# A windowed-attention and MLP kernel: one evacuation of k split by PSUM bank, small matmul groups and two stores put at other places

## The chip, the cores and the metric

The kernel runs on one core of a Trainium2 chip. Its engines have an instruction stream each and run side by side, held together by semaphores: PE (TensorE, matrix products into PSUM), DVE (VectorE), ACT (ScalarE), POOL (GpSimd) and SP (SyncE, which here issues every DMA). PSUM has eight banks of 512 fp32 values in each of 128 partitions. The metric is the device time of one execution in microseconds (us); lower is better.

## The reference

All data is bf16, S = 2048 rows of D = 512. `A` is attention in which each row sees itself and seven earlier rows two apart, with 32 heads of 16; `B` is a mixer with an MLP of width 1376. Both start from the same normalised rows, and the outcome is `x + A * silu(B)`.

```python
xn = layernorm(x)
# A: windowed attention
qkv = (xn @ wqkv) -> q, k, v of 32 heads x 16
idx = pos[:, None] - 2 * arange(8)           # masked where negative
attn = softmax(einsum("bhsd,bhswd->bhsw", q, k[idx]) * 16**-0.5)
s = einsum("bhsw,bhswd->bhsd", attn, v[idx]).reshape(B, S, D) @ wo
# B: mixer and MLP
h  = gelu(layernorm(xn) @ w1)
hs = concat(quarters of h shifted by +1, -1, +2, -2 rows) @ w2
x1 = xn + hs
g  = silu(x1 + gelu(layernorm(x1) @ w3) @ w4)
out = x + s * g
```

## The kernel before

The rows are split by parity: p = 0 holds the even rows, p = 1 the odd ones, 1024 each, so that a window two rows apart becomes eight neighbours within one parity. The row chunks c = 0 to 3 have 512 rows (0 and 1 of parity 0, 2 and 3 of parity 1), and 16 row tiles of 128.

The order of the instructions is written out by hand; each engine takes its own in the order in which the program names them. The first part (to about 109 us) makes q, k, v, the mixer and the first MLP product for all chunks. PSUM banks 0 to 5 serve it as three pairs in turn (`pair`, L91): a pair is filled by eight products of PE (`proj`, L332, products on L337) and emptied by ACT or DVE, and PE needs the same pair again three pairs later.

`k_all` (L358) makes k. The scores later want k twice, once with the odd heads of each pair set to zero and once with the even ones, as alternate elements of one tile, `kM[..., e]` with e = 0, 1. So each pair of banks is copied out twice, with a mask `em[:, e]` as scale. On ACT both copies are L366. In one call, `k_all(2, (1,), both=False)` (L596), the copy e = 0 is on ACT and the copy e = 1 on DVE (L368). Behind that call stand `w1(2, 0)`, `w1(2, 1)` and `w1(3, 0)`, whose products are also on L337.

The second part (109 us to 181 us) runs the attention in 18 units (`for n in range(NU)`, L900), nine for each parity, each of 114 rows. A unit n consists of

- `scores(n)` (L640): 32 small products on PE (L647) into banks 0 to 3, then the Exp on ACT (L654);
- `band(n - 1)` (L656): the mask on DVE (L659), for most units one unit later;
- `values(n - 2)` (L664): 32 small products (L673) into bank 4 and 16 (L683) that sum the weights into bank 5, then a copy of bank 4 by ACT (L688). For n = 15 both `values(13)`, ahead of the scores, and `values(14)` are called, and from then on `values(n - 1)`;
- a share of about nine products of `g_w4` (L779, products on L785). This is the MLP's second product: 16 groups of 11 products into one bank, 6 or 7, and then taken up by DVE (L798) and ACT (L805, or L801);
- one small group of four products: `g_v` (units 0 to 7, products on L816, copied by ACT, L385) or `g_fin` (from unit 8, L826, products on L838). `g_fin` is the output projection of one row tile: ACT copies the bank (L845), DVE multiplies by the gate (L853) and adds x (L855), and every second tile SP stores 256 KB (`store`, L749).

`w4_take` (L885) hands out the w4 products: three calls in a unit, about a third of its quota `q` each. Where a w4 group ends inside the second or third call, the unit's small group (`extra`) is run there, and the next w4 group starts behind it. The final steps of a `g_fin` group (L853, L855) wait in `finals` and are flushed at the start of the next unit, in unit 16 in its middle. Its store waits in `stores`, and `flush_stores(n - 2)` issues what is at least two units old.

The weights of the softmax are inverted for batches of four units (`inverse`, L695). They go to DRAM (`write_rec`, L700, DMAs on L704), come back spread over the partitions (`read_rec`, L706, DMAs on L707) and are multiplied in by DVE (`apply`, L712, product on L720). The values of each unit are loaded by `load_va` (L633, DMA on L636) into one of three slots.

After unit 17: `values(17)`, the last eight w4 products, two expansions of the last inverses on PE (L726), their copies on ACT (L734), and then seven `g_fin` tiles of parity 1 one after the other (L984), each with its two DVE products, and six stores. Each of these loops ends with `flush_stores(n)`.

Of the kernel before, what the change touches and what calls it, by code (L numbers as in the profile page):

```python
# [8 lines left out]
AF = mybir.ActivationFunctionType  # L9
ALU = mybir.AluOpType  # L10
# [10 lines left out]
def kernel(  # L21
# [17 lines left out]
    PE, DVE, ACT, POOL, SP = nc.tensor, nc.vector, nc.scalar, nc.gpsimd, nc.sync  # L39

    def pin(ins):

        return tc.keep_in_program_order(ins)
# [6 lines left out]
    NF = (F + P - 1) // P  # L50
# [11 lines left out]
    NU = 2 * UP  # L62
# [19 lines left out]
    def b8(shape, name):  # L82
        return big.tile(shape, BF16, name=name, tag="b8")
# [32 lines left out]
    for h in range(2):  # L116
        pin(SP.dma_start(
            out=wqk_sb[:, :, h * D // 2 : (h + 1) * D // 2], in_=wqkv_v[:, :, h * D // 2 : (h + 1) * D // 2]
# [31 lines left out]
    em = const.tile([P, 2], F32, name="em")  # L150
# [62 lines left out]
    class Norm:  # L213
# [24 lines left out]
        def apply(self, lo, hi):  # L238
            for j in range(lo, hi):
                pin(DVE.tensor_scalar(  # L240
                    out=self.dst[:, j, :], in0=self.src[:, j, :], scalar1=self.mv[:, j, 0:1],
                    scalar2=self.rstd[:, j : j + 1], op0=ALU.subtract, op1=ALU.mult,
                ))
# [88 lines left out]
    def proj(c, a, w, rhs):  # L332
        pt = pair()
        for b in range(2):
            nt = 2 * a + b
            for dt in range(ND):
                pin(PE.matmul(  # L337
                    pt[:, b, :], lhsT=w[:, dt, nt * P : (nt + 1) * P], rhs=rhs[:, dt, :],
                    start=(dt == 0), stop=(dt == ND - 1),
                ))  # L340
        return pt

    def chunk(t, c):
        p, k = c // 2, c % 2
        return t[p][:, :, k * CH : (k + 1) * CH]
# [12 lines left out]
    def k_all(c, parts=(0, 1), both=True):  # L358

        p, k = c // 2, c % 2  # L360
        for a in parts:
            pt = proj(c, a, wqk_sb[:, :, D : 2 * D], chunk(xnT, c))
            for e in range(2):
                dst = kM[p][:, 2 * a : 2 * a + 2, 8 + k * CH : 8 + (k + 1) * CH, e]
                if e == 0 or both:
                    pin(ACT.activation(dst, pt, AF.Copy, scale=em[:, e : e + 1]))  # L366
                else:
                    pin(DVE.tensor_scalar(out=dst, in0=pt, scalar1=em[:, e : e + 1], scalar2=None, op0=ALU.mult))  # L368

    vn = {"n": 0}  # L370

# [214 lines left out]
    while vputs:  # L586
# [11 lines left out]
        out=w4_sb[:, 0 : NF - 1, :],  # L598
# [65 lines left out]
    def values(n):  # L664
        p, u = n // UP, n % UP
        if u == 0:
            oT[p] = b8([P, ND, MQ], f"oT{p}")
        pr = probs.pop(n)
        for dt in range(ND):
            for k in range(2):  # L670
                for rg in range(4):
                    x = (2 * dt + k) * QB
                    pin(PE.matmul(  # L673
                        O_ps[32 * rg : 32 * rg + 32, x : x + QB],
                        lhsT=va_r[:, n % NV, k, 32 * (4 * dt + rg) : 32 * (4 * dt + rg) + 32],
                        rhs=pr[:, rg, x : x + QB], start=True, stop=True, tile_position=(0, 32 * rg),
                    ))
        b = batch_of[n]
        lo, hi = batches[b]
        st = den_st if hi - lo == 4 else den_s2  # L680
        for dt in range(ND):
            for rg in range(4):
                pin(PE.matmul(  # L683
                    D_ps[32 * rg : 32 * rg + 32, :], lhsT=st[:, 4 * (n - lo) + dt, :],
                    rhs=pr[:, rg, dt * NQ : (dt + 1) * NQ], start=(n == lo and dt == 0),
                    stop=(n == hi - 1 and dt == ND - 1), tile_position=(0, 32 * rg),
                ))
        pin(ACT.activation(  # L688
            oT[p][:, :, u * NQ : (u + 1) * NQ], O_ps[:, 0 : ND * NQ].rearrange("p (a q) -> p a q", q=NQ), AF.Copy
        ))  # L690
# [132 lines left out]
    stores = []  # L823
    now = {"n": 0}

    def g_fin(p, i, st=None, n=2, half=False, later=None, parts=1):  # L826

        W = D // parts
        sg = {}

        def one(pt, k):
            h, dt = k // ND, k % ND
            c = slice(h * W, (h + 1) * W)
            if dt == 0:
                sg["no"] = free.pop(0) if h else None
            if h:
                pt = PS[:, sg["no"], :]
            pin(PE.matmul(  # L838
                pt[:, 0:W], lhsT=oT[p][:, dt, i * P : (i + 1) * P], rhs=wo["sb"][:, dt, c],
                start=(dt == 0), stop=(dt == ND - 1),  # L840
            ))
            if dt == ND - 1:
                if h == 0:
                    sg["t"] = fin.tile([P, D], BF16, name="sg", tag="f")
                pin(ACT.activation(sg["t"][:, c], pt[:, 0:W], AF.Copy, scale=2.0 if half else 1.0))  # L845
                if h:
                    free.append(sg["no"])

        def done(pt):
            t = sg.pop("t")  # L850

            def steps():
                pin(DVE.tensor_tensor(out=t, in0=t, in1=xn[p][:, i, :], op=ALU.mult))  # L853
                x_o = xo[p][:, i, :]
                pin(DVE.tensor_tensor(out=x_o, in0=t, in1=x_o, op=ALU.add))  # L855
                if st is not None:
                    stores.append((now["n"], lambda: store(st, p, i + 1 - n, n)))

            if later is None:
                steps()  # L860
            else:
                later.append(steps)

        return Group(ND * parts, one, done)
# [10 lines left out]
    def flush(q):  # L875
        while q:
            q.pop(0)()

    def flush_stores(n):
        while stores and stores[0][0] <= n:  # L880
            stores.pop(0)[1]()

    open_w4 = [g for g in w4s]

    def w4_take(k, extra=()):  # L885

        while k > 0 and open_w4:
            k -= open_w4[0].take(k)
            if open_w4[0].at == open_w4[0].n:
                open_w4.pop(0)  # L890
                if extra:
                    extra.pop(0).all()

    HEAD, LAST = 6, 8
    W4 = 16 * NF - LAST - HEAD
    given = 0
    xo_at = {9: (1, 0), 12: (1, 2), 13: (1, 4), 16: (1, 6)}
    ends = {5: 0, 9: 1, 13: 2, 16: 3}
    load_va(0)
    for n in range(NU):  # L900
        now["n"] = n
        q = W4 * (n + 1) // NU - given
        given += q
        extra = small_g.get(n, [])
        if n == 0:
            w4_take(HEAD)

        for j in range(2):
            if n == NU - 1:
                read_rec(3, 2 * j, 2)  # L910
            elif n - 1 - j in ends:
                read_rec(ends[n - 1 - j], 2 * j, 2)
        if n == 15:
            values(13)
        scores(n)
        if 1 <= n < 16:
            band(n - 1)
        if n >= 2 and n != 15:
            values(n - 2 if n < 16 else n - 1)
        if n + 1 < NU:  # L920
            load_va(n + 1)
        if n == 4:
            load_wo()
        if n != 16:
            flush(finals)
        if n in ends:
            recs[ends[n]] = inverse()
            write_rec(ends[n])
        if n == 17:
            free += [2, 3]  # L930
            pin(ACT.preload_act_table_set("silu_and_others"))
        w4_take(q // 3)
        late = list(gates)
        gates.clear()
        flush(tanhs)
        if n == 15:
            apply(2, 0, 2)
        if n == 17:
            band(n)
        w4_take(q // 3, extra)  # L940
        if n < 15:
            flush(late)
        if 15 <= n < 17:
            band(n)
        if n == 16:
            flush(finals)
        if n == 15:
            values(14)
        w4_take(q - 2 * (q // 3), extra)
        for j in range(2):  # L950
            if n < 15 and n - 2 - j in ends:
                apply(ends[n - 2 - j], 2 * j, 2)
        if n == 16:
            apply(2, 2, 2)
        if n >= 15:
            flush(late)
            flush(gates)
        while extra:
            extra.pop(0).all()

        flush(vstores)
        if n in xo_at:
            load_xo(*xo_at[n])
        if n != 15:
            flush_stores(n - 2)

    n = NU
# [4 lines left out]
        apply(3, j, 2)  # L972
    flush(gates)
    flush(tanhs)
    w4_take(LAST)
    flush(tanhs)
    banks = [PS[:, i, :] for i in range(2)]
    for j in range(2):
# [4 lines left out]
        apply_kept(NU - 2 + j, kept[j])  # L983
    for i in range(1, 8):  # L984
        g_fin(1, i, (SP if i % 2 or i == 6 else None), 1 if i >= 6 else 2, half=i >= 5, parts=1 if i < 4 else 2).all()
        flush_stores(n)


# [28 lines left out]
```

## Time and profile before

| | us |
|---|---|
| three runs: median, lowest, highest | 193.91, 193.33, 194.72 |
| the profiled execution: device time | 194.53 |
| the profiled execution: span in the trace | 192.6 |
| last matmul of PE ends | 188.0 |
| last DVE product ends | 189.8 |
| last store is issued | 189.8 |

How to read the profile: it is one execution. The page gives each engine's busy time, the DMA queues, and the costliest groups by source line, with the idle time just ahead of them and what ended it ("issue" is time in which the profile shows nothing that the engine waited for). The views of the trace used below are the timeline (start, duration, engine, line, operation, output and inputs, count of merged instructions, and in brackets the idle time ahead of the row with its releaser), the waits (engine, line, releaser: total us, times, longest), and the windows (for a stretch of time, the busy us and the count of PE, PE's weight load, DVE, ACT and POOL, then the granted clock of PE, the DMA engines' busy share and GB/s).

In the first part and the units, the costliest groups are these (busy us, mean ns of one):

| group | count | us | ns |
|---|---|---|---|
| PE L479, w3 | 176 | 38.3 | 379 |
| PE L785, w4 | 176 | 46.2 | 380 |
| ACT L654, Exp | 18 | 30.4 | 1688 |
| ACT L366, copies of k | 15 | 19.5 | 1400 |
| DVE L659, mask | 18 | 19.9 | 1103 |
| DVE L368, copy of k | 1 | 1.4 | 1361 |

Products of PE overlap; one of 512 columns follows the other every 0.216 us.

### The profile page before, as it was taken

What the parts mean: (1) busy time and instruction counts of PE and PEld (TensorE: products, weight loads), DVE (VectorE), ACT (ScalarE), POOL (GpSimd) and SP (SyncE); (2) the same over time, 40 slices, a digit from 0 to 9 for tenths busy, and PEclk for the clock granted to TensorE, in tenths of its full rate; (3) what the DMA queues carried; (4) which work ended last, traced back from release to release, by engine and by line L of the source; (5) the groups of instructions that cost most, each with busy time, mean ns of one, the idle gap of its engine ahead of it and who ended that gap; (6) DMA issues with size and microseconds to landing.
All of it is one profiled execution on the core that took longest, in us unless ns stands there. A gap on an engine that the chain in (4) does not pass through costs nothing.

```text
span 192.6 us, 5267 instructions
## 1 busy us (share of the span) xinstructions
PE 185.7 (96%) x2244; PEld 90.2 (47%) x2244; DVE 114.5 (59%) x226; ACT 132.2 (69%) x152; POOL 20.4 (11%) x60
## 2 busy tenths in 40 slices
PE   7999999999999999999999999999999999989990
PEld 2464444444444444444444444544454555444570
DVE  5897783222562996665000045665579789779694
ACT  7299858977268246165656788787778878876881
POOL 3025653000020022042000000000000000000000
PEclk9999999999999999999999999999999999999997
DMA  4999574589704113514700045357653753744724
GB/s 138 326 359 296 132 150 95 95 258 340 238 0 82 32 29 64 104 27 83 223 25 0 26 144 161 108 165 239 212 161 78 220 195 84 205 115 101 226 74 149
DMA packets 39859, 27.74 MB, mean 144 GB/s; under 512 B 18068, under 2 KB 39324, under 8 KB 39836
## 3 DMA queue, kind: packets, MB, share of 16 engines
q1 hardware_dynamic: 39836, 27.41, 51.9%
q8 instruction: 17, 0.28, 0.6%
q14 instruction: 6, 0.05, 0.1%
HBM read 17.14 MB, written 6.59 MB: 123 GB/s over the span
## 4 chain that ended last, share of the span: by engine, by line
PE 75%; ACT 8%; DMA 6%; DVE 6%; issue 1%; SPq 1%
PE PS L479 20%; PE PS L785 18%; PE PS L337 14%; ACT kM L366 7%; PE PS L439 5%; PE PS L816 4%; PE PS L838 3%; PE PS L673 3%; PE PS L647 3%; PE PS L374 3%; DMA ring<-rec_d 3%; DMA xn<-in_A_x_dram 2%; PE PS L683 2%; DVE sg L853 2%; DMA rec_d<-rec 1%
## 5 line engine op out<-in xcount | busy, mean ns | idle before, releaser
L479 PE MATMUL PS<-x1nT,w_sb 128*128 128x512 bf16 (+1 forms) x176 | 38.3, 379 | 0.0
L654 ACT ACTIVATE prob<-PS 128x1824 bf16<-128x1824 f32 x18 | 30.4, 1688 | 4.4 <-PE PS L647 3.6
L785 PE MATMUL PS<-w_sb,h3a 128*128 128x512 bf16 x128 | 32.7, 380 | 0.0
L485 ACT ACTIVATE h3a<-PS 128x1024 bf16<-128x1024 f32 x16 | 16.4, 1025 | 20.6 <-PE PS L479 20.6
L798 DVE TENSOR_TENSOR xn<-PS,xn 128x512 bf16<-128x512 f32 x15 | 10.3, 687 | 31.8 <-PE PS L785 31.5
L479 PEld LDWEIGHTS <-w_sb 128*128 128x128 bf16 (+1 forms) x176 | 17.6, 100 | 20.4
L337 PE MATMUL PS<-xnT,wqk_sb 128*128 128x512 bf16 x112 | 25.0, 379 | 0.1
L366 ACT ACTIVATE kM<-PS,em 128x1024 bf16<-128x1024 f32 x15 | 19.5, 1400 | 2.2 <-PE PS L337 2.1
L659 DVE TENSOR_TENSOR prob<-prob,maskb 128x1824 bf16<-128x1824 bf16 x18 | 19.9, 1103 | 1.3 <-ACT prob L654 1.3
L785 PEld LDWEIGHTS <-h3a 128*128 128x128 bf16 x128 | 11.3, 97 | 13.4 <-issue 1.2
L337 PEld LDWEIGHTS <-wqk_sb 128*128 128x128 bf16 x112 | 10.9, 98 | 13.2 <-issue 0.3
L838 PE MATMUL PS<-wo_sb,oT 128*128 128x512 bf16 (+1 forms) x80 | 15.5, 336 | 0.0
L447 DVE TENSOR_TENSOR xn<-PS,xn 128x1024 bf16<-128x1024 f32 x8 | 9.6, 1214 | 9.6 <-PE PS L439 9.6
L337 PE MATMUL PS<-xn2T,w_sb 128*128 128x512 bf16 x64 | 14.6, 379 | 0.2 <-DVE kM L368 0.2
L439 PE MATMUL PS<-w_sb,hT 128*128 128x512 bf16 x64 | 14.5, 379 | 0.1
L845 ACT ACTIVATE sg<-PS 128x512 bf16<-128x512 f32 (+1 forms) x20 | 10.1, 512 | 6.2 <-PE PS L838 5.9
L785 PE MATMUL PS<-w_sb,h3b 128*128 128x512 bf16 (+1 forms) x48 | 13.5, 381 | 0.0
L385 ACT ACTIVATE vst<-PS 128x512 bf16<-128x512 f32 (+1 forms) x12 | 8.9, 738 | 5.3 <-ACT sig L805 3.0
L412 ACT ACTIVATE hT<-PS 128x1024 bf16<-128x1024 f32 x8 | 8.0, 1028 | 5.6 <-PE PS L337 5.6
L224 DVE BATCH_NORM_STATS2 l1s<-xn 128x6 f32<-128x512 bf16 x16 | 10.2, 679 | 1.3 <-DMA xn<-in_A_x_dram 1.3
L838 PEld LDWEIGHTS <-oT 128*128 128x128 bf16 x80 | 7.8, 98 | 6.2 <-issue 0.3
L224 DVE BATCH_NORM_STATS2 l3s<-xn 128x6 f32<-128x512 bf16 x16 | 10.2, 683 | 0.2
(105 smaller groups left out, 221.8 us busy)
## 6 DMA issues: line engine op xcount, KB each, us to landing
ring<-v_d SPq DMA_DIRECT2D x18, 256.0 KB, 3.0
v_d<-vst SPq DMA_DIRECT2D x16, 256.0 KB, 3.1
xo<-in_A_x_dram SPq DMA_DIRECT2D x8, 256.0 KB, 3.6
ring<-rec_d SPq DMA_DIRECT2D x8, 228.0 KB
out_dram<-xo SPq DMA_DIRECT2D x7, 256.0 KB, 6.6
xn<-in_A_x_dram SPq DMA_DIRECT2D x6, 256.0 KB, 4.7
w_sb<-in_B_w_dram SPq DMA_DIRECT2D x1, 1376.0 KB
w_sb<-in_B_w_dram SPq DMA_DIRECT2D x1, 1280.0 KB
```

What stands on the lines that cost most here:

```text
L224: pin(DVE.bn_stats(out=self.st[:, j, :], in_=self.src[:, j, :]))
L337: pin(PE.matmul(pt[:, b, :], lhsT=w[:, dt, nt * P : (nt + 1) * P], rhs=rhs[:, dt, :], start=(dt == 0), stop=(dt == ND - 1),))
L366: pin(ACT.activation(dst, pt, AF.Copy, scale=em[:, e : e + 1]))
L439: pin(PE.matmul(pt[:, j, :], lhsT=w2_src(p, g, m0), rhs=w2_sb[:, g, :], start=(g == 0), stop=(g == ND - 1),))
L479: pin(PE.matmul(pt[:fs, ft % 2, :], lhsT=w3_sb[:, dt, ft * P : ft * P + fs], rhs=x1nT[:, dt, :], start=(dt == 0), stop=(dt == ND - 1),))
L485: pin(ACT.activation(t[:, o : o + 2, :], pt, AF.Gelu_apprx_tanh))
L654: pin(ACT.activation(pr, S_ps[:, :, 0 : ND * NQ], AF.Exp, scale=SCALE))
L659: pin(DVE.tensor_tensor(out=f, in0=f, in1=maskb[:], op=ALU.min))
L785: pin(PE.matmul(pt, lhsT=h3_of(c, ft)[:fs, jj * P : (jj + 1) * P], rhs=w4_sb[:fs, ft, :], start=(ft == 0), stop=(ft == NF - 1 and silu < 2),))
L798: pin(DVE.tensor_tensor(out=x_i, in0=pt, in1=x_i, op=ALU.add))
L838: pin(PE.matmul(pt[:, 0:W], lhsT=oT[p][:, dt, i * P : (i + 1) * P], rhs=wo["sb"][:, dt, c], start=(dt == 0), stop=(dt == ND - 1),))
L845: pin(ACT.activation(sg["t"][:, c], pt[:, 0:W], AF.Copy, scale=2.0 if half else 1.0))
```

## The change

Four edits, in one step:

1. In the call of `k_all` with `both=False`, the copies are split by bank and not by e: ACT copies the first bank of the pair for e = 0 and for e = 1, DVE the second.
2. In unit 15, `values(14)` is called behind the first share of w4 products and not behind the second.
3. `w4_take` has a budget for the unit (`unit["left"]`). In units 0 to 7, if a w4 group has ended, its `g_v` group has run, and three or fewer products of the unit's budget are left, the unit ends there, and what is left goes into the next unit's quota. From unit 8 on, the `g_fin` group no longer runs where a w4 group ends, but at the end of the unit, after the w4 shares. Up to unit 16, if the w4 group open at that point has between one and four products done, it is first taken on to five.
4. In unit 17 no stores are flushed. In the end's loop, after tile 1, its store is put at the head of the list, so that the two stores of xo0 still in the list come behind it.

On the engines' queues this gives: on PE, another order of the groups in units 1, 2, 6 to 8, 11 to 13 and 15 to 17, with the same instructions; on DVE, two copies of 128x512 in place of one of 128x1024, and the second half of the product with the weights of batch 2 (L720) ahead of L853 and L855 of the last parity-0 tile; on ACT, two copies of 128x512 in place of one of 128x1024; on SP, the first xo1 store ahead of the last two xo0 stores, behind the two L707 reads of the last batch.

```diff
@@ -362,10 +362,12 @@
             pt = proj(c, a, wqk_sb[:, :, D : 2 * D], chunk(xnT, c))
             for e in range(2):
                 dst = kM[p][:, 2 * a : 2 * a + 2, 8 + k * CH : 8 + (k + 1) * CH, e]
-                if e == 0 or both:
-                    pin(ACT.activation(dst, pt, AF.Copy, scale=em[:, e : e + 1]))
+                sc = em[:, e : e + 1]
+                if both:
+                    pin(ACT.activation(dst, pt, AF.Copy, scale=sc))
                 else:
-                    pin(DVE.tensor_scalar(out=dst, in0=pt, scalar1=em[:, e : e + 1], scalar2=None, op0=ALU.mult))
+                    pin(ACT.activation(dst[:, 0], pt[:, 0], AF.Copy, scale=sc))
+                    pin(DVE.tensor_scalar(out=dst[:, 1], in0=pt[:, 1], scalar1=sc, scalar2=None, op0=ALU.mult))

     vn = {"n": 0}

@@ -882,28 +884,40 @@

     open_w4 = [g for g in w4s]

+    unit = {"left": 0, "given": 0}
     def w4_take(k, extra=()):

+        k = min(k, unit["left"])
         while k > 0 and open_w4:
-            k -= open_w4[0].take(k)
+            t = open_w4[0].take(k)
+            k -= t
+            unit["left"] -= t
+            unit["given"] += t
             if open_w4[0].at == open_w4[0].n:
                 open_w4.pop(0)
                 if extra:
                     extra.pop(0).all()
+                    if unit["left"] <= 3:
+                        k = unit["left"] = 0

     HEAD, LAST = 6, 8
     W4 = 16 * NF - LAST - HEAD
-    given = 0
     xo_at = {9: (1, 0), 12: (1, 2), 13: (1, 4), 16: (1, 6)}
     ends = {5: 0, 9: 1, 13: 2, 16: 3}
     load_va(0)
     for n in range(NU):
         now["n"] = n
-        q = W4 * (n + 1) // NU - given
-        given += q
+        q = W4 * (n + 1) // NU - unit["given"]
         extra = small_g.get(n, [])
+        early = n < 8
         if n == 0:
+            unit["left"] = HEAD
             w4_take(HEAD)
+            unit["given"] = 0
+        unit["left"] = q

         for j in range(2):
             if n == NU - 1:
@@ -934,19 +948,21 @@
         gates.clear()
         flush(tanhs)
         if n == 15:
+            values(14)
             apply(2, 0, 2)
         if n == 17:
             band(n)
-        w4_take(q // 3, extra)
+        w4_take(q // 3, extra if early else [])
         if n < 15:
             flush(late)
         if 15 <= n < 17:
             band(n)
         if n == 16:
             flush(finals)
-        if n == 15:
-            values(14)
-        w4_take(q - 2 * (q // 3), extra)
+        w4_take(q - 2 * (q // 3), extra if early else [])
+        if not early and n < NU - 1 and 0 < open_w4[0].at < 5:
+            unit["left"] = 5 - open_w4[0].at
+            w4_take(unit["left"])
         for j in range(2):
             if n < 15 and n - 2 - j in ends:
                 apply(ends[n - 2 - j], 2 * j, 2)
@@ -961,7 +977,7 @@
         flush(vstores)
         if n in xo_at:
             load_xo(*xo_at[n])
-        if n != 15:
+        if n != 15 and n < NU - 1:
             flush_stores(n - 2)

     n = NU
@@ -972,7 +988,8 @@
         apply(3, j, 2)
     flush(gates)
     flush(tanhs)
-    w4_take(LAST)
+    unit["left"] = 16 * NF
+    w4_take(16 * NF)
     flush(tanhs)
     banks = [PS[:, i, :] for i in range(2)]
     for j in range(2):
@@ -983,6 +1000,8 @@
         apply_kept(NU - 2 + j, kept[j])
     for i in range(1, 8):
         g_fin(1, i, (SP if i % 2 or i == 6 else None), 1 if i >= 6 else 2, half=i >= 5, parts=1 if i < 4 else 2).all()
+        if i == 1:
+            stores.insert(0, stores.pop())
         flush_stores(n)


```

## The prediction

> **What bounds the kernel now.** I read the page first: which engine is busy, and from when to when.
>
> ```profile
> PE 185.7 (96%) x2244; PEld 90.2 (47%) x2244; DVE 114.5 (59%) x226; ACT 132.2 (69%) x152; POOL 20.4 (11%) x60
> ...
> q8 instruction: 17, 0.28, 0.6%
> ```
>
> PE (TensorE) is busy 96% of a span of 192.6 us, so only what makes PE wait, or what lies behind its last matmul, can be worth anything. The second view is therefore the waits of PE from 12 us on: two in all.
>
> ```profile
> PE PS L673 <- issue: 0.5, 1, 0.5
> PE PS L337 <- DVE kM L368: 0.2, 1, 0.2
> ```
>
> The timeline shows the second of them, at 46 us. ACT's third copy of k (L366) ends at 44.92 (42.29 + 2.63), DVE's one copy (L368) starts only then and ends at 46.32, and PE, which wants that pair of PSUM banks again, starts 0.21 us late:
>
> ```profile
> 42.29 2.63 ACT L366 ACTIVATE kM<-PS,em 128x1024 bf16<-128x1024 f32 x2
> ...
> 44.96 1.36 DVE L368 TENSOR_SCALAR kM<-PS,em 128x1024 bf16<-128x1024 f32 x1 [3.17 <-ACT kM L366]
> ...
> 46.38 0.38 PE L337 MATMUL PS<-xn2T,w_sb 128*128 128x512 bf16 x1 [0.21 <-DVE kM L368]
> ```
>
> The timeline of PE shows the first, in unit 16: values(15) runs 21 of its 32 products, stops for 0.53 us with no releaser, then runs the other 11. All 32 read one loaded tile and one PSUM bank, so no data can have arrived between the 21st and the 22nd.
>
> ```profile
> 168.26 0.42 PE L673 MATMUL PS<-prob,ring 128*32 128x57 bf16 x32
> 168.51 0.39 PE L683 MATMUL PS<-prob,den_st 128*32 128x114 bf16 x16
> 168.83 0.82 PE L785 MATMUL PS<-w_sb,h3a 128*128 128x512 bf16 x3
> 169.49 1.03 PE L838 MATMUL PS<-wo_sb,oT 128*128 128x512 bf16 x4
> 170.45 0.40 PE L647 MATMUL PS<-qT,kM 32*128 32x57 bf16 x32
> 170.78 0.35 PE L673 MATMUL PS<-prob,ring 128*32 128x57 bf16 x21
> 171.66 0.27 PE L673 MATMUL PS<-prob,ring 128*32 128x57 bf16 x11 [0.53 <-issue]
> ```
>
> Last, the end. DVE waits 1.10 us for the read of the last weights (L707), then has no idle time until its last product at 189.80. The last store is issued at 189.83 and the span ends 2.8 us later.
>
> ```profile
> 176.52 1.24 SPq L707 DMA_DIRECT2D ring<-rec_d  x2
> ...
> 177.81 12.37 SPq L749 DMA_DIRECT2D out_dram<-xo  x7
> ...
> 181.52 1.31 DVE L720 TENSOR_TENSOR oT<-oT,ring 128x912 bf16<-128x912 bf16 x2 [1.10 <-DMA ring<-rec_d]
> ```
>
> The windows of 1 us say what room the DMA engines have there (the last two columns are their busy share and GB/s):
>
> ```profile
> 180.00:181.00 1.00, 1.00 (x7) 0.44 (x5) 0.42 (x1) 1.00 (x3) 0.00 (x0) 1.00 1.00 344
> ...
> 186.00:187.00 1.00, 1.00 (x12) 0.89 (x10) 0.93 (x4) 0.89 (x3) 0.00 (x0) 1.00 0.76 254
> 187.00:188.00 1.00, 1.00 (x10) 0.69 (x7) 0.97 (x3) 0.90 (x3) 0.00 (x0) 1.00 0.46 152
> 188.00:189.00 1.00, 0.04 (x1) 0.00 (x0) 0.97 (x4) 0.40 (x2) 0.00 (x0) 1.00 0.36 119
> 189.00:190.00 1.00, 0.00 (x0) 0.00 (x0) 0.77 (x3) 0.00 (x0) 0.00 (x0) 1.00 0.86 287
> ```
>
> **Part 1, the copies of k.** One ACT copy of 1024 columns (2.63 / 2 = 1.31 us) and one DVE copy (1.36) become two of 512 on each. The two engines then write different blocks of kM, where now they write alternate elements of one, so DVE need not wait for ACT. A 512-column copy from PSUM takes ACT 0.60 where 1024 take 1.025 (L796 and L348), so splitting adds about 0.17: ACT ends at 45.1 instead of 44.92. The next ACT copy, of hT, slips by that; the one after it waits 0.41 us for PE anyway and hides it, and without that cover it would cost 0.17. DVE can start when PE fills the second bank, about 42.8, and with two of 0.69 (L798, 512 columns) ends near 44.2. The pair is free at 45.1, and PE wants it at 46.17: 1.07 us of room. PE then waits for nothing until 171 us, so the 0.21 us passes on whole: **-0.21**.
>
> **Part 2, values(14) of unit 15.** It moves from behind six w4 products to behind three, so 3 x 0.216 = 0.65 us more of w4 lies between it and values(15). PSUM bank 4, into which it writes, must first be emptied of values(13): ACT's copy there (L688) runs from 166.62 to 167.16, and values(14) would start near 167.6, so 0.4 us is left; ACT's own order is unchanged. SP's load of the values for unit 17 waits on values(14) and goes out 0.65 us earlier; it is read at 178.87, 10 us on, which hides it either way. What becomes of the 0.53 us? Bounds: it stays (0), or goes (-0.53). More than the whole of it would need a further idle stretch, and there is none; a new stop elsewhere is bounded by the same row, +0.53. The packet records of the trace show what sort of stop it is: queue q8 moves 17 packets of 16 KB, and one of them starts at 169.13 and takes 1.19 us, to 170.32, just ahead of the stop. Twelve of them start between 115 and 173 us and only this one has an idle PE behind it; it is also where PE issues its small products most densely (values(13), scores(15), values(14), scores(16) and values(15) within 5.2 us). I read it as PE running out of fetched instructions. Moving 0.65 us of large, slow products in between is more than the 0.53 that lacks, if the fetch is asked for while values(14) runs; it changes nothing if it is asked for earlier. The start at 169.13 is right behind values(14), and I take the first: **-0.53**.
>
> The Trainium skill (Runtime: NRT & Kernel Launch, Instruction fetch mechanics) says that the sequencer fetches the next 16 KiB block, 256 instructions, while it runs the present one, and that crossing a boundary is mostly hidden. By that rule this stop is no fetch and the term is 0, a sum of -0.21. The packet size agrees with the trace; that it is hidden holds for eleven of the twelve.
>
> **Part 3, other places of the small groups.** In units 1 to 7 a unit ends with its g_v group when three or fewer w4 products are left: units 1, 6 and 7 hand 2, 3 and 1 products to the next. From unit 8 on, the g_fin group goes behind up to five products of the next w4 group; this changes units 11 to 13 (1 and 2 products more, 3 fewer), 16 and 17. PE's sum is the same. The covers: a unit shortened by 0.65 us to about 3.25 still holds the Exp of its scores (1.69), which frees the banks for the next; if it did not, up to 0.65 us would be lost. Unit 13, about 3.05 us long, gives ACT less than the 3.5 us of work that it has there (Exp 1.69, L688 0.55, L805 0.63, L845 0.60); PE needs none of these results before the next unit, so a lag of 0.4 us is covered. In unit 12 the copy of the group (L845, 0.60) comes just ahead of the Exp of unit 13 and may delay it by 0.1; the mask on it runs a unit later. In unit 16 five products (1.08 us) go ahead of the group, its copy ends near 175.7, and the Exp of unit 17 starts at 175.6 where it now starts at 175.55. On DVE the group's two products (L853, L855) now come behind the second half of L720 for batch 2 (0.62, its weights landed long before) and run from 176.2 to 177.05, ahead of the mask on unit 17, which waits for the Exp until 177.27 anyway; values(17) comes 0.49 us behind that mask's end. In unit 17 the group ends 0.65 us later, near 178.8; ACT takes it at 179.53 whatever happens. **0**.
>
> **Part 4, stores.** The two xo0 stores that SP now issues at 177.81 and 178.4, behind the L707 reads, move behind the first xo1 store, at 185.06. Two effects. (a) The reads may land sooner. At most the 1.10 us of DVE idle goes; but ACT's last copy ends at 188.46 (184.64 + 3.82), so DVE cannot end before 188.46 + 0.42 + 0.45 = 189.35 instead of 189.80: -0.45 at most. At least nothing: in the packet records the reads' packets take 200 ns on average from 178.75 to 179.25, with no store packet beside them, and 77 to 94 ns from 180.25 to 181, with the stores running. The stores do not slow them there; I take **0**. The Trainium skill (DMA: Bandwidth & Descriptors, Queues, rings and completion order) has it that each DMA engine consumes one queue's descriptors in ring order, so that a later store cannot get ahead of an earlier read. That gives 0 as well, and speaks against this part. (b) 512 KB more in the last 7 us: at 344 GB/s one store takes 0.76 us, two 1.52. Idle DMA time from 186 to 189 is 0.24 + 0.54 + 0.64 = 1.42 us, and 0.14 follows; SP needs 1.09 us to issue both (0.58 + 0.51), between the end of the xo1 issue at 185.43 and the next at 186.65. It fits, barely: **0**, with +1.52 if nothing is absorbed, and up to +3.8 if the last store lands in the 6.6 us that the table of issues gives as median for the stores, not in 2.8.
>
> **Sum.** -0.21 - 0.53 = -0.74. The profiled execution took 194.53 us (span 192.6 and 1.93 around it) and would take 193.8. It lies 0.62 above the median of the three runs, 193.91, which may mean that some of them lack the stop; against the median the sum gives **193.2 us**.
>
> **Rivals.**
> *The stop stays* (or is not in most runs): only 0.21 is won, 193.7. For it: the order changes nothing between scores(15) and the 21st product except what stands before what, and the fetch may have been asked for before values(14). Chance 0.28, and 0.07 that the k copies too bring nothing (193.9).
> *The reads land sooner as well*: -0.45 more, 192.7. For it: 176.52 to 181.52 is 5.0 us, where the loads of the values (ring<-v_d) land in 3.0. Against: the packet times above. Chance 0.17.
> *The parked stores hold up the last ones*: slower. Place: SP's queue and the DMA engines from 185 us on; price 1.52 with only the 0.21 won, 195.2; it decides from the point at which the idle DMA time ahead of 189 us falls under 1.52 us (by the rows it is 1.42), or SP issues the second xo0 store after 186.65. Chance 0.12; with the upper price 3.8 it gives 197.5.
> *Forecast* 193.2: chance 0.36.
>
> **Chances and range.** 1% (1.94 us) is about what a measurement here can tell from no change. All gains together are 1.19 us, so more than 1% faster (below 191.97) needs the full case and 0.7 more, such as the 0.6 by which the fastest run of before lies under its median: 0.07. More than 1% slower (above 195.85) is half of the case of the parked stores: 0.06, and I add 0.01 for a new stop of PE beside it. Within 1%: 0.86. The range goes from the full case less 0.3 of scatter, 192.4, to the case in which nothing is won, a new stop of 0.53 and 0.3 of scatter, 194.7.
>
> **What would show it.** Part 1: DVE's copies of k start before ACT's end, and the waits of PE lack the one on kM. Part 2: values(15) runs 32 products in one row; if a split row remains there, the first rival holds. Part 3: no new PE wait in the units. Part 4: DVE's idle time before L720 stays near 1.1 us, and from the last issue to the end it stays at 2.8 us; 4 or more would be the parked stores. The forecast is wrong if PE gets a new wait of over 0.5 us, or if the end grows.

## The result, and the profile after

| | before | after |
|---|---|---|
| median of 17 runs each, us | 194.0 (193.06 to 195.1) | 192.72 (192.32 to 194.13) |
| ratio | | 0.9946 (95%: 0.9923 to 0.9969) |
| the profiled execution, us | 194.53 | 192.94 |
| its span, us | 192.6 | 190.8 |

The changed kernel is faster by 0.54%, some 1.05 us; a second set of runs beside other kernels gave 0.9929 (0.9903 to 0.9955). The forecast was 193.2 us, 0.74 less than 193.91, the median of the three runs known then.

The page of the changed kernel, its first lines. Of the 2244 matmul records 29 are missing in this trace, so PE's share is a little low and its list of waits is full of gaps that are only missing records.

```profile
span 190.8 us, 5243 instructions
...
PE 181.4 (95%) x2215; PEld 90.2 (47%) x2244; DVE 114.4 (60%) x227; ACT 131.7 (69%) x153; POOL 20.2 (11%) x60
```

The weight loads (PEld) are all there. Counted from the start of the first weight load of each piece, to PE's last product, DVE's last product and the end of the span, the time divides as follows (us). The third column is a second profile of the changed kernel, the run e12 below.

| stretch | before | after | again |
|---|---|---|---|
| start to w1(2, 0) | 42.33 | 41.75 | 41.93 |
| w1(2, 0) to w2(0): 24 products | 5.55 | 5.18 | 5.18 |
| to scores(0) | 62.27 | 62.27 | 62.26 |
| scores(0) to values(13) | 55.80 | 55.52 | 55.50 |
| values(13) to scores(16) | 4.48 | 4.48 | 4.48 |
| scores(16) to scores(17) | 4.61 | 4.24 | 4.32 |
| scores(17) to PE's end | 12.98 | 12.98 | 12.98 |
| PE's end to DVE's end | 1.77 | 1.61 | 1.65 |
| DVE's end to the end of the span | 2.79 | 2.77 | 2.77 |

The first row is no gain of the change: nothing is changed there, and over the eight other profiles of kernels with an unchanged start it lies anywhere from 41.93 to 43.00. What the change moved is 0.37 at the copies of k, 0.28 in the units to 13 and 0.37 in unit 16. The 0.16 (0.12 in the second profile) by which DVE ends sooner behind PE is not shown to be the change's: over all fourteen profiles this stretch lies anywhere from 1.34 to 1.82, and it is 1.34 in e2 and e3 below, whose stores stand where they stood before.

The timeline of the changed kernel at the copies of k. DVE's two copies (L370) start at 42.24, right behind the products, and the pair is free when ACT ends at 44.46 (42.95 + 1.51), long before PE wants it:

```profile
41.71 1.39 ACT L367 ACTIVATE kM<-PS,em 128x1024 bf16<-128x1024 f32 x1
...
42.24 1.47 DVE L370 TENSOR_SCALAR kM<-PS,em 128x512 bf16<-128x512 f32 x2 [1.00 <-PE PS L337]
...
42.95 1.51 ACT L369 ACTIVATE kM<-PS,em 128x512 bf16<-128x512 f32 x2
```

The weight loads of values(15). The stop is still there, behind the 20th load of 32, and shorter:

```profile
169.53 0.21 PEld L675 LDWEIGHTS <-ring 128*32 128x32 bf16 x20
170.12 0.15 PEld L675 LDWEIGHTS <-ring 128*32 128x32 bf16 x12 [0.37 <-issue]
```

The end, in the timelines of SP's queue and of DVE. The first read of the last weights is issued at 174.83 and the stores come from 183.30 on, none right behind the reads any more:

```profile
174.83 1.24 SPq L709 DMA_DIRECT2D ring<-rec_d  x2
183.30 5.11 SPq L751 DMA_DIRECT2D out_dram<-xo  x7
```

Even so L722, the old L720, starts 5.03 us after that issue, as before (5.00), and DVE waits for the read:

```profile
179.86 1.21 DVE L722 TENSOR_TENSOR oT<-oT,ring 128x912 bf16<-128x912 bf16 x2 [1.05 <-DMA ring<-rec_d]
```

The windows show the DMA engines busy nearly without pause from 185 us on. In windows of 0.2 us they are still fully busy (1.01 and 1.04) up to 188.4, behind the issue of the last store at 188.06, and nearly idle (0.09) from 188.6 to 188.8; so the backlog of the parked stores was gone only just in time. The span still ends 2.8 us behind DVE:

```profile
180.00:181.00 1.00, 1.00 (x11) 0.57 (x9) 1.00 (x3) 1.00 (x3) 0.00 (x0) 1.00 0.00 0
...
185.00:186.00 1.00, 1.00 (x12) 0.90 (x10) 0.95 (x3) 0.86 (x3) 0.00 (x0) 1.00 0.99 326
186.00:187.00 1.00, 0.42 (x4) 0.13 (x2) 0.94 (x3) 0.77 (x2) 0.00 (x0) 1.00 1.01 356
187.00:188.00 1.00, 0.00 (x0) 0.00 (x0) 0.97 (x3) 0.00 (x0) 0.00 (x0) 1.00 0.93 303
188.00:189.00 1.00, 0.00 (x0) 0.00 (x0) 0.03 (x1) 0.00 (x0) 0.00 (x0) 0.74 0.65 217
```

### The profile page after: what moved, and what is told of

It is laid out like the page before. It is cut to its first block, busy times and chain, and to the rows that moved or that the text cites. A ratio compares the mean times of both kernels' runs of the same rounds, so it can differ in the third digit from the quotient of the medians.

```text
span 190.8 us, 5243 instructions
## 1 busy us (share of the span) xinstructions
PE 181.4 (95%) x2215; PEld 90.2 (47%) x2244; DVE 114.4 (60%) x227; ACT 131.7 (69%) x153; POOL 20.2 (11%) x60
## 4 chain that ended last, share of the span: by engine, by line
PE 77%; DVE 7%; ACT 6%; DMA 5%; issue 2%; SPq 0%
PE PS L481 20%; PE PS L787 17%; PE PS L337 16%; PE PS L441 5%; ACT kM L367 5%; PE PS L818 4%; PE PS L840 3%; PE PS L675 3%; PE PS L649 3%; PE PS L376 3%; DMA ring<-rec_d 3%; PE PS L685 2%; DVE sg L855 2%; DVE xo L857 1%; DVE l1s L224 1%
## 5 line engine op out<-in xcount | busy, mean ns | idle before, releaser
L787 PE MATMUL PS<-w_sb,h3a 128*128 128x512 bf16 x112 | 29.3, 379 | 1.6 <-issue 1.3
L800 DVE TENSOR_TENSOR xn<-PS,xn 128x512 bf16<-128x512 f32 x15 | 10.3, 685 | 31.7 <-PE PS L787 31.4
L367 ACT ACTIVATE kM<-PS,em 128x1024 bf16<-128x1024 f32 x14 | 18.3, 1402 | 2.2 <-PE PS L337 2.1
L787 PE MATMUL PS<-w_sb,h3b 128*128 128x512 bf16 (+1 forms) x44 | 12.8, 380 | 0.8 <-issue 0.8
```

Of the source, the lines that this page charges most:

```text
L367: pin(ACT.activation(dst, pt, AF.Copy, scale=sc))
L787: pin(PE.matmul(pt, lhsT=h3_of(c, ft)[:fs, jj * P : (jj + 1) * P], rhs=w4_sb[:fs, ft, :], start=(ft == 0), stop=(ft == NF - 1 and silu < 2),))
L800: pin(DVE.tensor_tensor(out=x_i, in0=pt, in1=x_i, op=ALU.add))
```

## The experiments

### Each part alone

Four kernels, each the kernel before with one part of the change.

**e1, the copies of k.**

```diff
-                if e == 0 or both:
+                if both:
                     pin(ACT.activation(dst, pt, AF.Copy, scale=sc))
                 else:
-                    pin(DVE.tensor_scalar(out=dst, in0=pt, scalar1=sc, scalar2=None, op0=ALU.mult))
+                    pin(ACT.activation(dst[:, 0], pt[:, 0], AF.Copy, scale=sc))
+                    pin(DVE.tensor_scalar(out=dst[:, 1], in0=pt[:, 1], scalar1=sc, scalar2=None, op0=ALU.mult))
```

> Part 1 alone (k copies split by bank). Theory: from the first product of w1(2, 0) to the first of w2(0), 24 products, PE takes 5.55 us before and 5.18 after; so 5.18 here, -0.37 us in that stretch and nothing elsewhere, a ratio near 0.998. Rival (the prediction's size): only the idle time that the waits name goes, 0.21, so 5.34. Second rival: the DVE copies still wait for ACT, 5.55. The units from 109 us on keep the order of before, so the seams and the stop in unit 16 should stay as before.

The stretch is 5.18, as the theory has it. All ten profiles with this part show 5.18, and the four without it (the kernel before, e2, e3 and e4) show 5.55 to 5.57. The ratio, 1.0001 (0.9968 to 1.0034), can't show 0.2%. And a stop that the kernel before did not have in its profile turned up in scores(15), in the weight loads of this run, while the one in values(15) was only 0.17 us:

```profile
165.87 0.20 PEld L649 LDWEIGHTS <-kM 32*128 32x128 bf16 x19
166.58 0.17 PEld L649 LDWEIGHTS <-kM 32*128 32x128 bf16 x13 [0.51 <-issue]
```

**e2, values(14) of unit 15.**

```diff
         if n == 15:
+            values(14)
             apply(2, 0, 2)
...
-        if n == 15:
-            values(14)
         w4_take(q - 2 * (q // 3), extra)
```

> Part 2 alone (values(14) behind three w4 products). Theory (PE runs out of fetched instructions, and the fetch is asked for before values(14)): the time from the first product of values(15) to the first product that sums its weights, 0.93 us before and 0.33 without a stop, stays between 0.6 and 0.95, because the order between the fetch and the stop is nearly the same. Rival (the prediction: the fetch is asked for while values(14) runs): the stop goes, 0.33 to 0.4, and the time falls by up to 0.6 us. Everything before 165 us as before.

The stop in values(15) stays: 0.66 to the weight sums, 0.44 more than without a stop (0.22; the 0.33 of the expectation was the length of the 32 products in another count). In scores(15) there is another of 0.60. Together 1.04 us, where the kernel before has 0.71. Ratio 1.0007 (0.9978 to 1.0035). Moving values(14) does not by itself take the stop away.

**e3, the small groups.** The budget in `w4_take`, the groups at the units' ends from unit 8 on, and the rule of five products, without the other three edits.

> Part 3 alone (small groups at other places of a unit). Theory: scores that come directly behind a small group start about 0.08 us sooner than scores behind w4 products that stand behind a small group; units 1, 6, 7, 12 and 16 lose such a piece of w4, so PE gains about 0.4 us between the first scores and the last, of which 0.28 before values(13). Rival (the prediction): the same products in another order take the same time, 0. The stretch of the k copies stays 5.55 and the stop in unit 16 is there in some size.

From scores(0) to values(13) 55.53, where e1, e2, e4 and the kernel before have 55.80 to 55.99. It is the only part whose time shows by itself: ratio 0.9963 (0.9937 to 0.999), 0.2 to 1.2 us. In this run PE did not stop in scores(15) or within values(15), but waited 0.7 us ahead of values(15) for the load of the values of that unit.

**e4, the stores.**

```diff
-        if n != 15:
+        if n != 15 and n < NU - 1:
             flush_stores(n - 2)
...
+        if i == 1:
+            stores.insert(0, stores.pop())
         flush_stores(n)
```

> Part 4 alone (two xo0 stores behind the first xo1 store). Theory (as predicted): the last reads of weights are issued and land as before, 5.0 us from the first issue to the first L720, and DVE's idle time ahead of it stays 1.0 to 1.1 us; the stores fit into idle DMA time and the end stays 2.8 us behind the last store's issue: ratio 1.000. Rival A (the reads land sooner): the wait falls to 0 to 0.6, and DVE ends up to 0.45 sooner. Rival B (parked stores hold up the last ones): the end comes 3.5 us or more behind the last issue.

The reads take 4.38 us to the first L720 and DVE waits 0.37. That is inside rival A's range; but e2 and e3, whose stores stand where they stood before, show 4.49 and 4.47, and the changed kernel 5.03 and 4.99 in its two profiles with the stores moved. The time from issue to use scatters from 4.4 to 5.0 with the stores in either place. The end stays 2.79 us behind DVE. Ratio 1.0013 (0.9982 to 1.0044): no effect.

### The stop in unit 16: do its place and its length belong to the data or to the instructions?

Numbered from 0 at the start of the program, the weight load at which a stop ended is the 2001st or 2002nd for values(15), and the 1875th (in e7 the 1874th) for scores(15). From one to the other are 127 weight loads, 127 products and two semaphore instructions: 256 instructions of PE. Three kernels add small products to the warm-up, so that all that follows has another number.

```diff
+    for i in range(64):           # 52 in e6, 8 in e10
+        r = 32 * (i % 4)
+        pin(PE.matmul(
+            PS[r : r + 32, 6, 0:57], lhsT=ones_bf[:, 0:32], rhs=ones_bf[:, 0:57],
+            start=True, stop=True, tile_position=(0, r),
+        ))
```

**e5, 64 products.**

> The changed kernel with 64 small products (128 instructions of PE) added to the warm-up at the start, in time in which PE waits for x. Nothing near unit 16 is changed. Theory: PE stops only where a block of 256 of its instructions begins, when the block has not been fetched; the stops seen so far lie at its 2002nd and 1875th weight load, which are 256 instructions apart. So the 21st product of values(15) runs without a stop (0.33 us to the weight sums instead of 0.66 to 0.93), and the block boundaries fall at values(13) and into the weight sums of unit 14, 128 instructions sooner. Between these two PE needs only some 2.0 us without a stop, where a fetch takes 4.3 to 4.9 from one boundary to release: a stop of 1.5 to 2.9 us in the sums of unit 14 (L685), and a time about 1 to 2.5 us above the changed kernel's. Rival (the stop belongs to the data or the place: a load, a bank, a semaphore): it stays at the 21st product of values(15), 0.3 to 0.7 us, and the time is the changed kernel's.

One half held and the other failed. The 32 products of values(15) run through, and scores(16) to scores(17) takes 3.81 us instead of 4.24:

```profile
169.93 0.30 PEld L681 LDWEIGHTS <-ring 128*32 128x32 bf16 x32
170.15 0.24 PEld L691 LDWEIGHTS <-den_st 128*32 128x32 bf16 x16
```

But the large stop that I expected in the weight sums of unit 14 is not there: the gap at the 2002nd weight load, 167.17 us, is 0.05. In the packet records the 16 KB packet for it starts at 164.72, 0.4 us before PE runs the first instruction of the block ahead of it (165.12); in the changed kernel the packet before the stop starts 2.1 us after that point (167.48 and 165.39). So the request is not tied to PE's products reaching the block before. The ratio is 0.9939 (0.9915 to 0.9964).

**e6, 52 products.**

> The same with 52 small products (104 instructions). Theory: the boundaries fall at the end of values(13)'s neighbourhood (164.8 us in the changed kernel's trace) and into scores(16) (169.2), 4.4 us apart, and 3.8 us apart at units 11 to 12. The stop moves from values(15) into scores(16) and is 0 to 0.5 us; one of 0 to 0.6 may come in scores(12) or values(12). Time between the changed kernel's and 0.5 us below it. Rival (place or data): the stop stays in values(15).

3.81 us again, no stop in scores(16), values(15) or the units 11 and 12; ratio 0.995 (0.9925 to 0.9975). That 0.43 us less in the units doesn't show in the time of either. In the four profiles with added products the start takes 42.14 to 42.74 us, which is inside the 41.75 to 43.00 of the unchanged starts, so no cost of the added products is shown there.

**e10, 8 products**: the test whether such additions move the stop or only take it away. (e10 and e9 ran once each, so only their traces are used.)

> The changed kernel with 8 small products (16 instructions of PE) added to the warm-up. Theory (a stop comes where a block of 256 PE instructions begins, and the request for it goes out when PE's sequencer, which runs some instructions ahead of its products, enters the block before it): with 16 instructions more ahead of it the boundary falls on the 13th product of values(15) instead of the 21st, and the boundary before on the 12th of scores(15); both are still in dense stretches, so the stop stays, 0.2 to 0.7 us, behind 12 or 13 products of values(15). Rival 1 (any such addition takes the stop away, as 52 and 64 did): no stop. Rival 2 (the stop belongs to the 21st product): it stays there.

The stop ends again at the 2001st weight load of the program, which is now the 13th of values(15) and not the 21st:

```profile
170.59 0.15 PEld L681 LDWEIGHTS <-ring 128*32 128x32 bf16 x12
170.96 0.21 PEld L681 LDWEIGHTS <-ring 128*32 128x32 bf16 x20 [0.22 <-issue]
```

A second one, of 0.6 us, ended at the 1619th weight load, which is three blocks of 256 instructions earlier. Both rivals fall: the place goes with the number of the instruction, not with the data, and an addition does not take the stop away unless the boundary comes to lie elsewhere. It is code loading: the Trainium skill (Runtime: NRT & Kernel Launch, Instruction fetch mechanics) has blocks of 256 instructions, and the trace agrees. That crossing a boundary is mostly hidden holds too: of the 17 or 18 packets of 16 KB in a profile, at most three have a stop behind them (e2, with a third one of 0.19 us in unit 8). But all the stops came in the dense small products or, as the second one of e10, at a large product right behind them, and they cost 0.2 to 0.7 us each. The packets also show why scores(15) stopped in some runs: in e1, e2, e4 and e7 the packet ahead of that block took 1.90 to 2.24 us, in the other profiles with the same boundary 0.94 to 1.46, or 1.88 in the kernel before, where it ended just in time. What made it slower is open.

### The units: what part 3 gained

**e7, one w4 product behind the small group.** From e3 I had read 0.08 us at each place where scores stand behind w4 products and these behind a small group, and put it down to that order.

```diff
         while extra:
             extra.pop(0).all()
+        if 8 <= n <= 16 and n != 11:
+            unit["left"] = 1
+            w4_take(1)
```

> The changed kernel with one w4 product moved from ahead of the small group to behind it in units 8 to 10, 12 to 14 and 16 (and 15), so that the next scores come behind w4 instead of a finished group. Theory: 0.08 us more in each unit that scores follow, so from the first scores to values(13) 55.5 + 5 x 0.08 = 55.9, and 0.08 more each into scores(16) and scores(17): about 0.5 us in all, ratio to the changed kernel 1.003. Rival (order of equal products costs nothing, and the gain of part 3 came from elsewhere): 55.5, no change.

The time rose (ratio 0.9994, 0.9967 to 1.002, where the changed kernel has 0.9946), but not as expected. From scores(0) to values(13) it is 56.22, 0.70 more than in the changed kernel; 0.22 of that is one product more in the stretch, and 0.52 stand in unit 13 alone, where the profile names the cause (unit 9 takes 0.15 less, unit 10 0.12 more). In units 8, 12, 15 and 16 the same order cost nothing. The theory of the order fell. The timeline of unit 13 in this run:

```profile
161.17 1.03 PE L840 MATMUL PS<-wo_sb,oT 128*128 128x512 bf16 x4
...
161.83 0.68 DVE L800 TENSOR_TENSOR xn<-PS,xn 128x512 bf16<-128x512 f32 x1
...
162.56 0.38 PE L787 MATMUL PS<-w_sb,h3a 128*128 128x512 bf16 x1 [0.36 <-DVE xn L800]
```

PE waits for DVE to empty the bank (L800, the old L798), which comes late because DVE has the inversion of the weights (L697) and L809 ahead of it. With that in mind, the kernel before, in unit 1:

```profile
115.35 1.03 PE L816 MATMUL PS<-wv_sb,xnT 128*128 128x512 bf16 x4
115.55 0.69 DVE L798 TENSOR_TENSOR xn<-PS,xn 128x512 bf16<-128x512 f32 x1 [1.56 <-PE PS L785]
...
116.30 0.59 PE L785 MATMUL PS<-w_sb,h3a 128*128 128x512 bf16 x2
```

The small group takes the free one of banks 6 and 7; the next w4 group takes the one in which the last w4 group ended, 0.86 us later. L798 ends at 116.24, and the product starts at 116.30 where its turn was at 116.22. No idle time is printed: a product lasts 0.38 us in the records and the next one is due after 0.216, so a wait of up to 0.16 is hidden under the end of the product before. The weight loads show it: the second one of this group starts 0.295 us behind the first, not 0.216. Waits of this kind that the change leaves in place are 0.08 us in units 0 and 5 and 0.15 in unit 9.

**e9, without the rule of five products.**

```diff
-        if not early and n < NU - 1 and 0 < open_w4[0].at < 5:
-            unit["left"] = 5 - open_w4[0].at
-            w4_take(unit["left"])
```

> The changed kernel without the rule that takes the open w4 group on to five products. Only units 11 to 13 differ: in unit 12 the small group stands behind two products of the new w4 group, where it had five. Theory (the 0.08 us pieces and part 3's gain are PE waiting for a bank of 6 and 7 that DVE, on L800, has not emptied): the small group takes the bank of the w4 group that has just ended; L800 starts near 0.2 us behind that group's last product and takes 0.69, so the small group, due 0.65 us behind that product, waits some 0.5 us for DVE: from the first scores to values(13) 56.0 instead of 55.52, and the waits name DVE L800. Rival (what counts is only which kind of product comes just ahead of the scores): 55.5.

56.04, with the wait named where it was expected, so the bank is the cause:

```profile
155.91 0.59 PE L787 MATMUL PS<-w_sb,h3a 128*128 128x512 bf16 x2
156.11 0.69 DVE L800 TENSOR_TENSOR xn<-PS,xn 128x512 bf16<-128x512 f32 x1 [0.53 <-PE PS L787]
...
156.86 1.02 PE L840 MATMUL PS<-wo_sb,oT 128*128 128x512 bf16 x4 [0.35 <-DVE xn L800]
```

### The end: what holds up the reads

**e8, nothing ahead of the reads.** In the changed kernel.

```diff
-    xo_at = {9: (1, 0), 12: (1, 2), 13: (1, 4), 16: (1, 6)}
+    xo_at = {9: (1, 0), 10: (1, 6), 12: (1, 2), 13: (1, 4)}
...
-        if n != 15 and n < NU - 1:
+        if n < 15:
             flush_stores(n - 2)
+        if n == 17:
+            flush_stores(13)
```

> The changed kernel, with what SP issues just AHEAD of the last two reads of weights taken away from there: the last xo load goes to unit 10, the store of xo0 rows 2 and 3 behind the reads. Theory: reads are held up by what is ahead of them in SP's queue and not by what is behind; from the first read's issue to the first L722 it takes 3.0 to 3.7 us instead of 5.0, DVE's wait falls from 1.05 to 0, and DVE ends 1.34 us behind PE's last product instead of 1.61 (the value of the runs whose wait was under 0.5): 0.27 us won. Rival (the reads are slow in themselves, 4.4 to 5.0 whatever stands ahead): wait 0.4 to 1.1 as before, end 1.34 to 1.6 behind PE.

Mostly as the theory has it: 4.11 us instead of 5.03, less of a gain than expected, but DVE no longer waits for the reads (it is busy until then, so they may have landed sooner), and it ends 1.34 us behind PE. The run e11 below, with the same edit, also shows no wait (4.34 us, 1.34), while the other seven profiles in the changed order have waits of 0.87 to 1.24. What stands ahead is not all of it: in e2, e3 and e4, with the load and the store in place, the time was 4.38 to 4.49. The timeline of SP's queue, and that of DVE, where no wait is printed ahead of L722:

```profile
174.64 1.85 SPq L709 DMA_DIRECT2D ring<-rec_d  x2
176.53 0.58 SPq L751 DMA_DIRECT2D out_dram<-xo  x1
```

```profile
178.76 1.15 DVE L722 TENSOR_TENSOR oT<-oT,ring 128x912 bf16<-128x912 bf16 x2
```

A store right behind the reads is there again, and does no harm. Ratio 0.9909 (0.9874 to 0.9944), the lowest of all; its interval overlaps those of the changed kernel.

**e11 and e12, both edits together beside the changed kernel.** e11 is the changed kernel with e6's 52 products and e8's edits, e12 the changed kernel itself.

> The changed kernel with 52 small products in the warm-up and with the reads of weights ahead of the load and the store (both edits that won in the trace, together). Theory: no stop in unit 16 (scores(16) to scores(17) 3.81 us instead of 4.24) and DVE's end 1.34 us behind PE's last product instead of 1.61: 0.7 us below the changed kernel from the k products on; ratio to the kernel before 0.991 to 0.992 where the changed kernel has 0.9946. Rival (the two overlap, or the start pays for the added products): 0.994 or more.

> The changed kernel once more, for a second profile. Theory: the k stretch 5.18, from the first scores to values(13) 55.5, a stop of 0.2 to 0.7 us in values(15) (or in scores(15)), DVE's end 1.34 to 1.6 us behind PE's last product, the end 2.7 us behind DVE's last product; the start of w1(2, 0) anywhere from 41.7 to 42.4, whatever the kernel. Ratio 0.993 to 0.997.

In e11's trace both gains are there (3.81 us, 1.34 us), but its start took 42.74, and the ratio is 0.9923 (0.9899 to 0.9947) beside 0.9929 (0.9903 to 0.9955) for e12: no version here is shown to beat the changed kernel in time. e12 repeats the changed kernel's stretches, with 0.74 us to the weight sums of values(15) where the first profile has 0.66.

## Why the prediction was right, point by point

**The bound.** PE stayed the bound: the stretch from w2(0) to scores(0) is the same to 0.01 us, and what the change is shown to gain stands where PE waited.

**Part 1, -0.21: the mechanism held, the size was too small.** It is 0.37. The waits count PE's idle time from the end of the last product, and that end is a model's: 0.38 us behind its start, where the next product is due after 0.216. Add the 0.16 between them and 0.21 becomes 0.37. The cover named for the copy of hT held.

**Part 2, -0.53: the step failed.** The prediction took it that "the fetch is asked for while values(14) runs", so that moving values(14) takes the stop away. That the stop is a missing fetch is now shown by e10. But part 2 alone left 1.04 us of stops (e2). With the whole change 0.44 and 0.52 us remain, against 0.71 before, counted with the end of the products taken off: a gain of 0.27 and 0.19 instead of 0.53. The first comes out halfway between the 0.53 that the prediction took and the 0 that stood beside it by the Trainium skill's rule. The size hangs on the profiles compared: with the order of before, scores(15) and values(15) lose 0.71 to 0.78 us together (the kernel before, e1, e4); with the changed order e8 and e9 lose 0.23 and 0.26, e10 0.28 there beside its 0.6 in unit 12, and e7 0.92. A stop in scores(15) was seen in three of the four profiles with the old order that also have the old boundary, or nearly (e1, e2, e4, not the kernel before), and among those with the new order only in e7. Why the fetches came sooner there, and what sends a request out, stays open: e5 shows only that it is not PE's products entering the block before.

**Part 3, 0: the step failed.** "PE's sum is the same" left out the wait for the bank that the last w4 group ended in; the list of two waits, and with it "PE then waits for nothing until 171 us", hid it. In the old order the next group takes the bank 0.86 us after that group's last product, and emptying it takes DVE 0.69 and the handing over some 0.25 (0.2 ahead of it, 0.05 behind): 0.08 us too late, at the five places of units 1, 6, 7, 12 and 16 that the change removes. The stretch to values(13) shows 0.28 and unit 16 another 0.10 (0.37 less the 0.27 of the stop): 0.38 in all, the largest term of the change. The covers that the prediction did name (Exp, ACT's lag, the mask) held.

**Part 4, 0: right on both counts.** (a) The reads did not land sooner (5.03 and 4.99 against 5.00), though the time scatters from 4.4 to 5.0 with the stores in either place; taking away what stood ahead of them did help (e8, e11). By the Trainium skill (DMA: Bandwidth & Descriptors, Queues, rings and completion order) each DMA engine takes a queue's descriptors in ring order, and the trace agrees. The same section of the Trainium skill says that a later one may finish its write before an earlier one, so the prediction's "cannot get ahead" holds for the order in which they are taken, not for their ends. (b) The parked stores fitted, with little to spare: 2.77 us from DVE's end to the end of the span, where it was 2.79.

**The sum.** Forecast -0.74 against the median; measured -1.05 by the ratio. In the traces: 0.37 + 0.38 + 0.27 = 1.02 us, without the start and without the 0.16 for DVE's end, which is inside its scatter. That the sum came near is in part luck: one term was too large by 0.26 and two were too small, by 0.16 and 0.38. Of the rivals, that the stop stays holds by the sign that the prediction named for it, a split row of values(15), though the stop became shorter. The two about the stores and the reads were decided as the prediction had them.

## What to carry to other kernels

A PE wait in such a profile is longer than printed by the difference between a product's recorded length and the spacing of products, and waits shorter than that difference are not printed at all; compare the starts of equal work in the two traces. Where accumulating groups take turns in two banks, let the bank that has just ended rest for as long as its emptying takes (here some 0.94 us) before anyone takes it again. To bring a late DMA forward, look first at what was issued ahead of it, not behind.

## What was not expected of the hardware

PE can run out of instructions: in or right behind dense small products, 32 of them in some 0.3 us, it stopped for 0.2 to 0.7 us where a block of 256 instructions begins, and 16 instructions more at the start of the program moved the stop by 8 pairs of weight load and product. The 16 KB packet ahead of each stop ended 1.3 to 1.6 us before PE went on.
